# Layer 1 of a linear attention block: summing phi(K) on GpSimd and VectorE instead of TensorE

## The chip, the cores and the metric

The kernel runs on one core of a Trainium2 chip. A core has five engines with queues of their own, which work at the same time: TensorE (PE, matrix products), VectorE (DVE), ScalarE (ACT), GpSimd (POOL) and SyncE (SP, which here issues most transfers). An instruction waits for others through semaphores. The metric is the device time of one execution in microseconds (us).

## The reference

The input x has 2048 tokens of 512 values in bf16. Two layers follow each other with the same weights; each is an attention without softmax and then an MLP (F = 1792), and each of these normalises its input twice. Cut to what matters here:

```python
phi = lambda t: jnp.where(t > 0, t + 1, jnp.exp(t)) + 1e-6
pq, pk = phi(q), phi(k)                       # 32 heads of 16 values
kv = jnp.einsum("bhsd,bhse->bhde", pk, v)
z = jnp.einsum("bhsd->bhd", pk)               # sum over all 2048 tokens
num = jnp.einsum("bhqd,bhde->bhqe", pq, kv)
den = jnp.einsum("bhqd,bhd->bhq", pq, z)[..., None] + 1e-6
o = num / den                                 # then o @ wo, added to x
```

`z` is the one that the change concerns: for each of the 512 columns of phi(K), the sum over all tokens. Nothing can be divided by `den` before z is complete.

## The kernel before, in words

**Tiles and chunks.** The tokens form 16 tiles of 128 (one token per partition), and four chunks of four tiles. For each tile and layer there is a normalisation (`norm`: statistics on VectorE, a power on GpSimd, the scaling on VectorE or ScalarE), a transpose (by DMA or TensorE), and the K projection with phi (`attn_k`, L702). phi takes an exponential on ScalarE, often a relu on ScalarE too, a minimum on VectorE, and a sum or maximum on VectorE or GpSimd (L675 to L700). The result is a bf16 tile `pk` of 128 tokens by 512 columns, in one of eight buffers.

**The kv product** isn't formed from V. `attn_g_held` and `attn_g_chunk` (L767, L797) sum G, the product of phi(K) with the normalised tokens; `attn_kv` (L823) multiplies G with the V weights at the end of a layer's K phase, masks it to the heads, and multiplies it with the output weights (the M products, L853). `attn_out` (L911) then takes one product per tile of normalised phi(Q) with M.

**z** is summed in `attn_z` (L748), chunk by chunk: sixteen matmuls (L756) with a 128x128 block of a `pk` tile as the stationary operand and a single column of ones as the moving one. The PSUM result, four columns of 128 values, is copied to `zs` for chunk 0 (L762) and added to it for the others (L765). After the last chunk `zb` (L836) spreads `zs` over the head blocks for the denominators (the D matmuls, L899). In layer 1, chunks 2 and 3 divide in another layout ("tok"): for them the diagonal matrix `dz` (L841) and one matmul turn z into the row `zrow` (L788, L844).

**The order of the work** comes from a planner inside the kernel (`Scheduler`, L111). Every operation is recorded in a graph with an engine, a supposed duration in ns, a latency and a priority. The planner walks through time: for each engine it takes, of the operations that can start within a window, the one with the lowest priority value. The order it finds is then written out, engine by engine, with semaphore waits for the true dependencies, so each engine's queue is fixed. `CONF` (L348) holds the knobs: priorities by phase, `SHIFT` (additions to the priority of a group or of one operation), and `WAY` (which engine does an operation that two can do). Layer 0's MLP and layer 1's K phase are interleaved, so that TensorE has up and down projections (L955, L993) to do while tiles of layer 1 are normalised.

Of the kernel before, what the change touches and what calls it, by code (L numbers as in the profile page):

```python
# [5 lines left out]
FP32 = mybir.dt.float32  # L6
BF16 = mybir.dt.bfloat16
ACT = mybir.ActivationFunctionType
ALU = mybir.AluOpType
# [282 lines left out]
def assign_waits(graph, order, sems, dma_sems):  # L292
# [10 lines left out]
    while len(done) < total:  # L303
# [45 lines left out]
    N_HALF=1, N_K=3, N_Q=2, P_Z0=6.99, N_PB=1, N_PT=8, P_DEN=-45.12, P_A2=-16.36, P_W1=58.86, P_W2=84.95,  # L349
    P_K=47.92, P_G=125.74, P_Q=226.77, STEP=5.92, A1_Q=51.41, A1_STEP=3.23, N_H=4, N_N=2, GAP=9.92,  # L350
    TABLE_PENALTY=0.77, WINDOW=100.11,
    SHIFT={
        "B00_0": -215.0, "B00_1": -89.8, "B00_2": -26.6, "B00_3": 14.5, "B01": 170.5, "B02": 2.6,
        "B03": 342.3, "B10_0": 36.9, "B10_1": -0.2, "B10_2": 19.8, "B10_3": -16.6, "B11": 145.9, "B12": 147.7,
        "B13": 321.5, "D00": -7.7, "D01": 35.6, "D02": 71.3, "D03": 21.9, "D0_0_2": -0.8, "D0_1_3": 16.7,
        "D0_3_3": -9.4, "D10": -127.9, "D11": 5.4, "D13": 286.8, "G00_0": -37.7, "G00_1": 178.6,
        "G00_2": 70.8, "G00_3": 74.3, "G01_0": -71.1, "G01_2": -10.9, "G01_3": -70.8, "G02_0": 0.5,
        "G02_1": 195.0, "G02_2": 284.2, "G02_3": -6.8, "G03_0": 89.0, "G03_1": 18.3, "G03_2": -1.1,
        "G03_3": 584.1, "G0_0_0": 2.9, "G0_14_0": -60.7, "G0_2_0": -10.6, "G11": -2.0, "G12": 42.0,
        "G13": 28.8, "G1_1_1": -5.3, "K00_0": -245.9, "K00_1": -93.1, "K00_2": -888.1, "K00_3": -23.3,  # L360
        "K01_0": 22.0, "K01_1": 13.4, "K01_2": -187.7, "K02_1": 2.3, "K02_2": 74.6, "K02_3": -0.5,
        "K03_0": -39.1, "K03_1": -1.7, "K03_2": 123.4, "K03_3": 65.6, "K0_10": -82.3, "K10": 72.2,
        "K11": 53.6, "K12": 56.2, "K13": -41.5, "K1_1": 3.3, "K1_4": 9.5, "KV1_1": -5.4, "N00_0": -216.1,
        "N00_1": -271.1, "N00_2": -218.8, "N00_3": -3.7, "N01_0": -376.7, "N01_1": 8.9, "N01_2": -172.6,
        "N01_3": -2.9, "N02_0": -2.1, "N02_1": 63.3, "N02_2": 27.8, "N02_3": 71.9, "N03_0": 1.1,
        "N03_1": 125.2, "N03_2": 54.2, "N03_3": 25.0, "N10": -45.4, "N11": -2.3, "N13": 66.0, "O00_0": -143.2,
        "O00_1": -173.2, "O00_2": -44.0, "O00_3": -66.7, "O01": -57.3, "O02": -43.6, "O03": 41.2,
        "O10_0": -100.8, "O10_1": -47.6, "O10_2": -1.0, "O10_3": 63.4, "O11": -324.7, "O12": 0.7, "O13": 11.8,
        "OD6": 0.5, "PTA0_0": 0.7, "PTB0_2": 0.1, "Q00": 195.1, "Q01": 18.0, "Q02": 282.6, "Q03": 272.4,
        "Q10": 301.7, "Q11": -67.4, "Q12": 350.9, "Q13": 281.6, "RA1_1": 9.4, "RB0_7": -18.9, "RB0_8": -16.0,  # L370
        "RB1_1": 1.3, "TA1_6": 17.6, "TB1_8": 16.4, "U00_0": -318.5, "U00_1": -4.1, "U01": 10.6,
        "U02": -110.1, "U03": -42.4, "U10_0": -93.4, "U10_1": -26.8, "U11": -323.4, "U12": 153.7,
        "U13": 177.4, "V0": 52.4, "V1": -5.0, "W00": 6.8, "W01": 2.4, "W02": 2.5, "W03": -174.6, "W10": -38.7,
        "W10_0_10_1": -19.4, "W10_1_11_0": 4.2, "W10_2_13_0": 1.4, "W10_3_11_0": -1.7, "W11": -15.2,
        "W11_0_10_1": 3.7, "W11_0_7_0": -2.4, "W11_1_11_0": -7.7, "W11_1_7_0": 1.0, "W11_2_10_0": 46.6,
        "W11_2_2_0": 9.9, "W11_3_7_0": 3.6, "W12": -73.5, "W13": 161.9, "W20_0_0": -11.8, "W20_0_7": -1.2,
        "W20_10_7": -2.4, "W20_8_0": 0.7, "W21_12_7": 18.9, "W21_7_0": 2.2, "WO0_14_0": -4.0, "Z00": -51.5,
        "Z01": -33.6, "Z02": -104.9, "Z03": -6.4, "Z0_3": -19.5, "Z10": -0.8, "Z11": -29.8, "Z12": -111.3,
        "Z13": 2.4, "Z1_0": -3.1, "aggrA0_10": 19.5, "aggrA0_14": -16.8, "aggrA0_2": -1.3, "aggrA0_3": -2.0,
        "aggrB0_11": 3.9, "aggrB1_11": -10.5, "aggrB1_13": -0.3, "aggrB1_15": -0.8, "aggrB1_5": -3.4,  # L380
        "b20_14": -2.4, "b21_0": 3.7, "b21_13": -1.7, "b21_7": -2.8, "cpg0_0": 54.9, "expk1_10": 52.3,
        "expq0_0_3": 58.3, "expq0_1_1": 4.4, "expq1_1_0": 6.1, "expq1_2_0": -51.9, "ga1_2_1": 31.2,
        "gelu0_0_11_0": -7.1, "gelu0_0_11_1": 0.3, "gelu0_0_13_1": 2.4, "gelu0_0_1_0": 2.0,
        "gelu0_0_1_1": 1.8, "gelu0_0_4_0": -0.5, "gelu0_0_4_1": -6.4, "gelu0_0_9_1": 5.8, "gelu0_1_3_0": 7.4,
        "gelu1_0_11_0": -10.8, "gelu1_0_1_1": 3.0, "gelu1_0_6_1": -20.7, "gelu1_1_12_0": 17.2,
        "gelu1_1_8_0": 89.1, "gelu1_2_0_0": 3.3, "gelu1_3_12_0": 36.8, "gelu1_3_3_0": 16.3,
        "gelu1_3_8_0": -3.2, "ln0_1_0": 45.5, "ln1_1_2": -6.5, "minq0_0_3": 43.7, "minq0_1_1": -0.8,
        "minq1_0_2": 3.3, "normA0_4": -0.1, "normA1_9": -10.9, "normB0_12": 0.2, "normB0_13": -3.7,
        "normB0_5": 1.9, "normB0_6": 8.8, "phik0_2": -5.9, "phik1_0": -2.3, "phiq0_0_2": 7.1,
        "powA0_11": 16.1, "powA0_3": 1.3, "powA1_0": 7.6, "powA1_14": 7.5, "powA1_15": -2.7, "powA1_2": 1.9,  # L390
        "powB0_12": 20.6, "powB0_14": -34.9, "powB1_0": -14.6, "powB1_2": 17.9, "powB1_3": -7.9,
        "pr0_1_3": 2.5, "pr1_0_0": -6.8, "pr1_0_3": 9.4, "rec0_1_2": 40.6, "rec0_2_1": 58.8, "rec1_1_2": -0.9,
        "rec1_2_0": 16.6, "red1_2_3": 12.3, "reluk1_12": -1.4, "reluq0_0_1": -2.8, "reluq0_2_1": 10.4,
        "reluq1_0_0": -3.1, "statsA1_12": -5.4, "statsB0_13": -24.1, "statsB0_3": 37.2, "statsB0_6": -0.4,
        "statsB1_6": 45.8, "statsB1_7": -1.1, "vepsA0_0": -1.0, "vepsA0_12": -7.7, "vepsA0_14": -18.3,
        "vepsA0_5": 14.9, "vepsA1_12": -0.8, "vepsA1_4": 2.1, "vepsA1_8": -43.7, "vepsB1_12": 11.3,
        "vepsB1_14": 0.6, "vepsB1_3": -13.9, "vepsB1_4": -20.2, "vepsB1_5": 50.0, "vepsB1_6": -16.4,
        "w2_1": -0.9,
    },
    WAY={  # L400
        "TA0_0": "pe", "TA0_1": "pe", "TA0_10": "dma", "TA0_11": "pe", "TA0_12": "dma", "TA0_13": "dma",
        "TA0_14": "dma", "TA0_15": "dma", "TA0_2": "pe", "TA0_3": "pe", "TA0_4": "pe", "TA0_5": "pe",
        "TA0_6": "dma", "TA0_7": "pe", "TA0_8": "dma", "TA0_9": "dma", "TA1_0": "dma", "TA1_1": "dma",
        "TA1_10": "dma", "TA1_11": "pe", "TA1_12": "pe", "TA1_13": "dma", "TA1_14": "pe", "TA1_15": "dma",
        "TA1_2": "dma", "TA1_3": "dma", "TA1_4": "dma", "TA1_5": "dma", "TA1_6": "pe", "TA1_7": "pe",
        "TA1_8": "pe", "TA1_9": "dma", "TB0_0": "dma", "TB0_1": "pe", "TB0_10": "dma", "TB0_11": "dma",
        "TB0_12": "dma", "TB0_13": "dma", "TB0_14": "dma", "TB0_15": "dma", "TB0_2": "pe", "TB0_3": "dma",
        "TB0_4": "dma", "TB0_5": "dma", "TB0_6": "dma", "TB0_7": "dma", "TB0_8": "dma", "TB0_9": "dma",
        "TB1_0": "pe", "TB1_1": "dma", "TB1_10": "dma", "TB1_11": "dma", "TB1_12": "dma", "TB1_13": "dma",
        "TB1_14": "dma", "TB1_15": "dma", "TB1_2": "dma", "TB1_3": "dma", "TB1_4": "dma", "TB1_5": "dma",  # L410
        "TB1_6": "dma", "TB1_7": "dma", "TB1_8": "dma", "TB1_9": "dma", "b20_0": "dve", "b20_1": "pool",
        "b20_10": "dve", "b20_11": "pool", "b20_12": "dve", "b20_13": "pool", "b20_14": "dve",
        "b20_15": "dve", "b20_2": "pool", "b20_3": "dve", "b20_4": "pool", "b20_5": "dve", "b20_6": "pool",
        "b20_7": "pool", "b20_8": "pool", "b20_9": "pool", "b21_0": "pool", "b21_1": "pool", "b21_10": "dve",
        "b21_11": "dve", "b21_12": "pool", "b21_13": "dve", "b21_14": "pool", "b21_15": "pool",
        "b21_2": "dve", "b21_3": "pool", "b21_4": "dve", "b21_5": "dve", "b21_6": "dve", "b21_7": "pool",
        "b21_8": "dve", "b21_9": "pool", "cpg0_0": "dve", "cpg0_1": "dve", "cpg0_2": "dve", "cpg0_3": "act",
        "cpg1_0": "act", "cpg1_1": "act", "cpg1_2": "act", "cpg1_3": "act", "cpm0_0": "act", "cpm0_1": "dve",
        "cpm0_2": "dve", "cpm0_3": "act", "cpm1_0": "dve", "cpm1_1": "dve", "cpm1_2": "dve", "cpm1_3": "act",
# [36 lines left out]
def build_kernel(nc, A_x, A_wqkv, A_wo, B_x, B_w1, B_b1, B_w2, B_b2, out, conf=None, report=False):  # L456
# [5 lines left out]
    with ExitStack() as es:  # L462
# [36 lines left out]
        zb = SB("zb", [P, D], BF16)  # L499
        eps6 = SB("eps6", [P, 1], FP32)  # L500
        dz = SB("dz", [P, D], BF16)
        zrow = SB("zrow", [P, D], BF16)
        rd = SB("rd", [P, 4, H], FP32)
        rr = SB("rr", [P, 4, H], FP32)
        outb = SB("outb", [P, NOUT, D], BF16)
# [681 lines left out]
```

## Time and profile before

The time is 333.03 us, median of three runs (333.03 to 333.08). The profiled execution has a span of 331.0 us.

| engine | busy us | share | instructions |
|---|---|---|---|
| TensorE, matmuls | 324.7 | 98% | 1782 |
| TensorE, weight loads | 161.0 | 49% | 1782 |
| VectorE | 206.8 | 62% | 445 |
| ScalarE | 212.9 | 64% | 361 |
| GpSimd | 139.8 | 42% | 225 |

| group | count | busy us | mean ns |
|---|---|---|---|
| z matmuls, L756, 128 stationary columns, 1 moving column | 128 | 4.4 | 163 |
| TensorE transposes, L659 | 44 | 4.3 | 220 |
| kv products, L830 | 32 | 3.1 | 220 |
| `zs` sums on VectorE, L765 | 6 | 0.9 | 155 |
| fp32 addition of a 128x512 tile on GpSimd, L940 | 17 | 20.8 | 1230 |
| the same on VectorE, L940 | 15 | 10.7 | 719 |

Busy time is the time in which at least one of the group's instructions ran; the mean is that of a single one. Where matmuls overlap, the mean says more than one costs: 128 times 163 ns is 20.9 us, but the group was busy for 4.4. In the chain of work that ended last, each step is followed back to what released it, and its pieces are the time that each really added. TensorE's clock is full in all of the span.

### The profile page before, as it was taken

What the parts mean: (1) busy time and instruction counts of PE and PEld (TensorE: products, weight loads), DVE (VectorE), ACT (ScalarE), POOL (GpSimd) and SP (SyncE); (2) the same over time, 40 slices, a digit from 0 to 9 for tenths busy, and PEclk for the clock granted to TensorE, in tenths of its full rate; (3) what the DMA queues carried; (4) which work ended last, traced back from release to release, by engine and by line L of the source; (5) the groups of instructions that cost most, each with busy time, mean ns of one, the idle gap of its engine ahead of it and who ended that gap; (6) DMA issues with size and microseconds to landing.
All of it is one profiled execution on the core that took longest, in us unless ns stands there. A gap on an engine that the chain in (4) does not pass through costs nothing.

```text
span 331.0 us, 4842 instructions
## 1 busy us (share of the span) xinstructions
PE 324.7 (98%) x1782; PEld 161.0 (49%) x1782; DVE 206.8 (62%) x445; ACT 212.9 (64%) x361; POOL 139.8 (42%) x225
## 2 busy tenths in 40 slices
PE   7899999999999999999999999999999999999996
PEld 2444444587444444444444444448744444444444
DVE  6888848973769304997107669998899495302012
ACT  3786789999998883431940798969936521831820
POOL 6763544985847102575102642478623062600000
PEclk9999999999999999999999999999999999999999
DMA  8813750012112100212101010002332132201001
GB/s 267 272 35 67 258 201 1 18 32 50 33 35 42 21 16 2 48 32 50 32 0 34 16 32 4 1 16 50 68 77 63 32 70 75 48 2 61 4 11 54
DMA packets 40116, 18.42 MB, mean 56 GB/s; under 512 B 33756, under 2 KB 39132, under 8 KB 40092
## 3 DMA queue, kind: packets, MB, share of 16 engines
q1 hardware_dynamic: 36524, 10.90, 14.9%
q0 software_dynamic: 1056, 4.72, 4.0%
q10 hardware_dynamic: 2512, 2.49, 2.3%
q8 instruction: 14, 0.23, 0.3%
q14 instruction: 10, 0.08, 0.1%
HBM read 8.00 MB, written 2.10 MB: 31 GB/s over the span
## 4 chain that ended last, share of the span: by engine, by line
PE 93%; DVE 2%; ACT 1%; POOL 1%; DMA 1%; issue 1%
PE ps L955 29%; PE ps L993 28%; PE ps L923 8%; PE ps L710 6%; PE ps L741 6%; PE ps L807 4%; PE ps L775 3%; PE ps L728 2%; PE ps L899 2%; PE ps L756 1%; PE ps L980 1%; POOL rstd L623 1%; DMA t<-in_A_x_dram 1%; ACT eb L680 1%; DVE stats L611 1%
## 5 line engine op out<-in xcount | busy, mean ns | idle before, releaser
L961 ACT ACTIVATE gT<-ps,b1c 128x512 bf16<-128x512 f32 (+1 forms) x140 | 80.2, 603 | 38.8 <-PE ps L955 38.5
L955 PE MATMUL ps<-t,w 128*128 128x512 bf16 (+1 forms) x560 | 99.1, 336 | 0.0
L993 PE MATMUL ps<-w,gT 128*128 128x512 bf16 x434 | 97.6, 379 | 0.0
L955 PEld LDWEIGHTS ps<-t,w 128*128 128x128 bf16 x560 | 54.6, 98 | 43.3 <-ACT t L669 0.3
L993 PEld LDWEIGHTS ps<-w,gT 128*128 128x128 bf16 x434 | 42.4, 98 | 50.1
L680 ACT ACTIVATE eb<-ps 128x512 bf16<-128x512 f32 x64 | 38.4, 617 | 19.6 <-PE ps L710 16.4
L691 ACT ACTIVATE rb<-ps 128x512 bf16<-128x512 f32 x55 | 33.2, 623 | 15.5 <-PE ps L710 12.4
L623 POOL TENSOR_TENSOR rstd<-veps,neghalf 128x1 f32<-128x1 f32 x64 | 38.4, 601 | 6.6 <-DVE veps L621 1.9
L999 DVE TENSOR_TENSOR xsb<-ps,xsb 128x512 f32<-128x512 f32 x16 | 10.9, 682 | 39.0 <-PE ps L993 38.9
L1003 DVE TENSOR_TENSOR outb<-ps,xsb 128x512 bf16<-128x512 f32 x15 | 10.4, 692 | 38.4 <-PE ps L993 38.0
L611 DVE BATCH_NORM_STATS2 stats<-xsb 128x6 f32<-128x512 f32 x48 | 32.6, 680 | 0.6
L710 PE MATMUL ps<-wqkv,t 128*128 128x512 bf16 x128 | 31.6, 379 | 0.2 <-ACT t L669 0.2
L923 PE MATMUL ps<-gtb,t 128*128 128x512 bf16 x128 | 30.3, 379 | 0.0
L621 POOL TENSOR_SCALAR veps<-mv 128x1 f32<-128x1 f32 x29 | 7.7, 268 | 53.3 <-DVE mv L613 52.8
L631 ACT ACTIVATE yb<-xsb,nmr,rstd 128x512 bf16<-128x512 f32 x21 | 16.8, 811 | 20.0 <-POOL nmr L628 19.4
L907 POOL TENSOR_TENSOR t<-t,lr 128x512 bf16<-128x512 bf16 x15 | 18.1, 1212 | 16.5 <-ACT lr L903 16.5
L693 DVE TENSOR_SCALAR eb<-eb 128x512 bf16<-128x512 bf16 x55 | 20.0, 373 | 7.8 <-ACT eb L680 7.5
L741 PE MATMUL ps<-t,wqkv 128*128 128x512 bf16 x96 | 24.1, 379 | 0.0
L940 POOL TENSOR_TENSOR xsb<-xsb,b2b 128x512 f32<-128x512 f32 x17 | 20.8, 1230 | 6.3 <-ACT yb L631 3.5
L636 DVE TENSOR_SCALAR yb<-xsb,mv,rstd 128x512 bf16<-128x512 f32 x27 | 18.4, 681 | 7.8 <-POOL rstd L623 7.6
L923 PEld LDWEIGHTS ps<-gtb,t 128*128 128x128 bf16 x128 | 12.4, 98 | 15.7 <-DVE t L907 0.4
L710 PEld LDWEIGHTS ps<-wqkv,t 128*128 128x128 bf16 x128 | 12.2, 98 | 14.7 <-ACT t L669 1.0
(81 smaller groups left out, 362.2 us busy)
## 6 DMA issues: line engine op xcount, KB each, us to landing
w<-in_B_w_dram POOLq DMA_DIRECT2D x4, 896.0 KB, 7.5
out_dram<-outb SPq DMA_DIRECT2D x15, 128.0 KB, 1.7
t<-in_A_x_dram ACTq DMA_DIRECT2D x3, 512.0 KB, 8.0
t<-yb SPq DMA_TRANSPOSE x53, 2.4
wqkv<-in_A_wqkv_dram SPq DMA_DIRECT2D x1, 512.0 KB, 5.3
wqkv<-in_A_wqkv_dram ACTq DMA_DIRECT2D x1, 512.0 KB, 7.0
wqkv<-in_A_wqkv_dram POOLq DMA_DIRECT2D x1, 512.0 KB, 6.9
wo<-in_A_wo_dram POOLq DMA_DIRECT2D x1, 512.0 KB, 6.5
```

What stands on the lines that cost most here:

```text
L611: G.op("dve", lambda e: e.bn_stats(stats[:, s.slot, :], src()), 620, reads=src_keys, writes=[k + "s"], tiles=[s, *src_tiles], prio=prio, n ...
L623: G.op("pool", lambda e: e.tensor_tensor(rstd[:, s.slot:s.slot + 1], veps[:, s.slot:s.slot + 1], neghalf[:], op=ALU.pow), 570, reads=[k + ...
L680: G.op("act", lambda e: e.activation(eb[:, et.slot, :], bank(bt), ACT.Exp), 478, reads=[src_key], writes=[f"e{tag}"], tiles=[bt, et], prio ...
L691: G.op("act", lambda e: e.activation(rb[:, rt.slot, :], bank(bt), ACT.Relu), 478, reads=[src_key], writes=[f"r{tag}"], tiles=[bt, rt], pri ...
L693: G.op("dve", lambda e: e.tensor_scalar(eb[:, et.slot, :], eb[:, et.slot, :], 1.0, 1e-6, op0=ALU.min, op1=ALU.add), 210, reads=[f"e{tag}"] ...
L710: ins = e.matmul(bank(b), lhsT=yTa(yT)[:, dt, k * P:(k + 1) * P], rhs=wqkv[:, dt, D:2 * D], start=(dt == 0), stop=(dt == DT - 1))
L741: ins = e.matmul(bank(b), lhsT=wqkv[:, dt, kt * P:(kt + 1) * P], rhs=yTa(yT)[:, dt, :], start=(dt == 0), stop=(dt == DT - 1))
L923: ins = e.matmul(bank(wb), lhsT=yTa(pq)[:, kt, k * P:(k + 1) * P], rhs=gtb[:, kt, :], start=(kt == 0), stop=(kt == DT - 1))
L940: G.op("pool" if on_pool else "dve", lambda e: e.tensor_tensor(xsb[:, st, :], xsb[:, st, :], b2b[:], op=ALU.add), 1120 if on_pool else 600 ...
L955: ins = e.matmul(bank(b, n), lhsT=w1[:, dt, ft * P:(ft + 1) * P], rhs=yTa(yT)[:, dt, k0 * P:k1 * P], start=(dt == 0), stop=(dt == DT - 1))
L961: G.op("act", lambda e, ft=ft, b=b, k0=k0, k1=k1, n=n: e.activation(gT[:, g.slot, ft * 512 + k0 * P:ft * 512 + k1 * P], bank(b, n), ACT.Ge ...
L993: ins = e.matmul(bank(b), lhsT=gT[:, g.slot, ft * 512 + k * P:ft * 512 + (k + 1) * P], rhs=w2[:, ft, :], start=(ft == 0), stop=(ft == FT - 1))
```

## The change

In layer 1, z of the first three chunks (twelve tiles) no longer comes from TensorE tile by tile. The twelve `pk` tiles are added up in an fp32 tile `zacc` by eleven additions in series, `za1` to `za11`. `WAY` gives `za2`, `za3`, `za8`, `za10` and `za11` to GpSimd and the other six to VectorE. TensorE takes bf16 here, so VectorE then splits the sum in two bf16 tiles: `dz` is `zacc` rounded (the high half), and `zrow` is what the rounding left (the low half). These two tiles are free at that time. Eight one-column matmuls (`ZH`) sum both halves over the partitions, and one copy (`zsh`) puts the result into `zs`. Chunk 3 goes the old way and is added to it; so does all of layer 0. This is for taking matmuls away from TensorE.

```diff
 def attn_z(L, c, pks, prio):
     G.grp = f"Z{L}{c}"
+    if L == 1 and c < NC - 1:
+        for k in range(4):
+            st = 4 * c + k
+            if st == 0:
+                continue
+            on_pool = eng(f"za{st}") != "dve"
+            G.op("pool" if on_pool else "dve",
+                 lambda e, st=st, k=k: e.tensor_tensor(
+                     zacc[:], pkb[:, pk0s[0].slot, :] if st == 1 else zacc[:], pkb[:, pks[k].slot, :], op=ALU.add),
+                 1150 if on_pool else 600, reads=[f"pk1_{st}", "pk1_0" if st == 1 else "zacc"], writes=["zacc"],
+                 tiles=[pks[k]] + ([pk0s[0]] if st == 1 else []), prio=prio, name=f"za{st}", lat=60, fast=not on_pool)
+        if c < NC - 2:
+            return
+        G.op("dve", lambda e: e.tensor_scalar(dz[:], zacc[:], 1.0, None, op0=ALU.mult), 340, ..., name="zhi", ...)
+        G.op("dve", lambda e: e.tensor_tensor(zrow[:], zacc[:], dz[:], op=ALU.subtract), 600, ..., name="zlo", ...)
+        b = Tile(psum, "zh", "t")
+        def hfn(e):
+            for kt in range(DT):
+                for src in (dz, zrow):
+                    ins = e.matmul(bank(b)[:, kt:kt + 1], lhsT=src[:, kt * P:(kt + 1) * P], rhs=onesm[:, 0:1],
+                                   start=(src is dz), stop=(src is zrow))
+            return ins
+        G.op("pe", hfn, 300, reads=["dz", "zrow", "onesm"], writes=["zh"], tiles=[b], ..., name="ZH", lat=MM_DRAIN, n=8)
+        G.op("dve", lambda e: e.tensor_scalar(zs[:], bank(b)[:, 0:DT], 1.0, None, op0=ALU.mult), 130, ..., name="zsh", lat=40)
+        return
...
-    G.op("pe", fn, 400, reads=[f"pk{L}_{4 * c + k}" for k in range(4)] + ["onesm"], ...
+    G.op("pe", fn, 595, reads=[f"pk{L}_{4 * c + k}" for k in range(4)] + ["onesm"], ...
 def attn_kv(L, prio):
...
-        G.op("pe", fn, 220, reads=[("gt", dc), "wv"] + ...
+        G.op("pe", fn, 380, reads=[("gt", dc), "wv"] + ...
```

The last two lines change only what the planner supposes of the old z groups and of the kv products. `CONF` is replaced as a whole with it: nearly every priority, shift and choice of engine is new, so the order of all queues is another one. In counts by engine, apart from the new operations: ScalarE gets five more normalisations (28 for 23) and two more loads of its function tables (16 for 14), GpSimd loses six phi sums (17 for 23) and three residual additions (14 for 17) and gets three more products of the layer's denominators (18 for 15, L907), and VectorE gets what the others lose. The counts of all large matmuls and of TensorE transposes stay as they are. `N_H`, the number of up-projection results that the planner keeps in hand, goes from 4 to 2.

## The prediction

> **What bounds the kernel now.** I read the page first: busy time by engine and the chain that ended last. Then TensorE's waits, the busy time by stretch, and the chain in order of time where TensorE stops.
>
> ```profile
> PE 324.7 (98%) x1782; PEld 161.0 (49%) x1782; DVE 206.8 (62%) x445; ACT 212.9 (64%) x361; POOL 139.8 (42%) x225
> ...
> PE 93%; DVE 2%; ACT 1%; POOL 1%; DMA 1%; issue 1%
> ```
>
> TensorE is the bound: 98% busy and 93% of the chain. GpSimd has 191 us to spare, VectorE 124 us. So work taken from TensorE is worth its full length, and work added elsewhere is free as long as TensorE never waits for it.
>
> ```profile
> 5.62:16.13 10.51, 8.94 (x58) 4.19 (x57) 9.82 (x29) 7.21 (x14) 7.96 (x17) 1.00 0.98 305
> 16.13:39.00 22.87, 22.54 (x155) 10.95 (x153) 19.41 (x54) 17.92 (x36) 13.50 (x22) 1.00 0.35 91
> 39.00:54.00 15.00, 14.66 (x98) 7.00 (x95) 9.50 (x23) 12.94 (x24) 5.69 (x5) 1.00 0.47 171
> 54.00:199.00 145.00, 145.00 (x776) 71.79 (x775) 86.84 (x174) 102.02 (x169) 68.92 (x109) 1.00 0.14 28
> 199.00:213.00 14.00, 14.00 (x92) 7.00 (x91) 13.27 (x29) 12.14 (x22) 4.99 (x4) 1.00 0.01 2
> ```
>
> These are stretches (start and end, length, then busy time of TensorE, weight loads, VectorE, ScalarE, GpSimd). From 54 to 199 us TensorE has no gap at all, so only its amount of work counts there. Its few gaps lie in the head and where the layer-0 attention turns into its output.
>
> The chain in order of time gives the true price of each matmul, since pipelined durations overlap:
>
> ```profile
> 198.54 0.89 PE ps L807 x4
> 199.43 0.38 PE ps L756 x16
> 199.80 1.75 PE ps L807 x8
> 201.55 0.43 PE ps L899 x2
> ```
>
> A 512-column matmul takes 0.86/4 = 0.216 us. Sixteen one-column matmuls (L756, one chunk of z) take 0.38 us, and the block after them is 0.03 longer than the usual 0.86: 0.41 us, or 25.6 ns each.
>
> Now the sum. At 0.2158 us for 1315 matmuls of 512 columns, 0.109 for 252 of 256, 0.054 for 76 of 128 and 0.0256 for 128 of one column, the work after the warm-up is 318.8 us. It starts at 5.62 and ends at 328.5 us: 322.9 us, so 4.1 us are waits. About 2.25 lie before 16.13 us, 0.5 before the z matmuls at 38.59, 1.0 around the kv product (48 to 52 us), 0.3 in the second layer. A retuned order can win no more than these.
>
> **What the Trainium skill says.** "Perfetto Trace Analysis", section "Identifying the Most-Contended Engine": matmul busy time is a poor measure because matmuls are pipelined. The trace agrees: the L756 row says 163 ns each where the chain gives 25.6. "TensorE: Matmul & The Clock Gate", section "Back-to-back issue gap": 1 to 64 columns cost an issue floor of about 25 ns, and 512 columns 518 cycles (216 ns). The chain shows both. "SBUF — State Buffer", section "Who interferes with whom": a VectorE instruction with two SBUF inputs and a GpSimd instruction that reads SBUF lock each other out for a whole instruction. The trace agrees: the `dz` product (L841) took 1.64 us beside a GpSimd add running from 200.50 to 202.03, and the similar L836 took 0.68.
>
> **The change part by part.** *Removed:* three z groups of layer 1 (chunks 0 to 2), 48 one-column matmuls: 48 x 25.6 ns = 1.23 us of TensorE. *Added:* eight such matmuls for the high and low halves: 0.20. Net -1.03 us, all in a stretch without gaps, so it counts in full.
>
> *Added beside it:* eleven fp32 additions, five on GpSimd and six on VectorE. Their nearest rows:
>
> ```profile
> L940 POOL TENSOR_TENSOR xsb<-xsb,b2b 128x512 f32<-128x512 f32 x17 | 20.8, 1230 | 6.3 <-ACT yb L631 3.5 <-DVE yb L636 2.7
> L940 DVE TENSOR_TENSOR xsb<-xsb,b2b 128x512 f32<-128x512 f32 x15 | 10.7, 719 | 1.8 <-ACT yb L631 1.7
> ```
>
> That is 5 x 1.23 = 6.2 us of GpSimd and 6 x 0.72 = 4.3 us of VectorE. The rounding to `dz` is like L636 (fp32 in, bf16 out, median 0.55), the subtraction 0.72, and two small `zs` additions (0.15 each) go. VectorE gets about 5.3 us more, GpSimd 6.2. The matmuls from 100 to 199 us hide these: VectorE is 60% busy from 54 to 199, GpSimd 48%. A trace of before can't show lock-outs among the new additions; each is bounded by 0 and by one whole other instruction (1.2 us). They delay only the queue behind them, so I take 0 on TensorE and keep 1 us for the high end.
>
> *A new wait:* the eight matmuls wait for eleven additions in series, the rounding and the subtraction. In the changed instruction order they stand behind the last K projection, and the four K blocks that include tile 11 are well ahead. Between them lie 16 G, 16 Q, then 16 more matmuls of G, K, G and Q: 48 x 0.216 = 10.4 us. After the K of tile 11: exp and minimum 0.6 + 0.3, its phi addition 1.2, the last two sums 2.4, rounding and subtraction 1.3, some 6 us with semaphores. Slack about 4 us: no wait. Queued behind the eight are Q and G matmuls, with all TensorE behind them.
>
> *Moved:* the whole order, since priorities and engine choices are new (and the planner's costs of Z and KV are raised). Layer 0's end: the z wait of 0.5 us goes, as more K and Q matmuls stand before Z. The first kv product stands behind all G and one Q block, not between G matmuls, so its wait shrinks from 1.0 to some 0.2. Against that, the M products are followed at once by the output projection; a copy out of PSUM takes 0.69 us plus about 0.3 of drain and signals, with 0.87 us of matmuls between: up to 0.5 of wait. Net -0.8. Layer 1's end: all four copies of M are on VectorE (4 x 0.68 in series), which leaves the fourth some 0.4 us late: +0.3. In its favour, `dz` no longer has GpSimd phi additions queued beside it. VectorE, 95% busy from 199 to 213, may run late: 0 to 1.5 us, I take 0.2. Elsewhere ScalarE gets five more normalisations (0.81 each) less two evacuations (0.6 each), 2.8 us, and two more table loads (1.28 each); from 54 to 131 us it is already 67 of 77 us busy. I take no wait there and keep 1 us for the range. Head and tail keep their order nearly: 0.
>
> Sum: -1.03 - 0.8 + 0.3 + 0.2 = -1.3 us, so 333.03 - 1.3 = 331.7 us.
>
> **The rivals.** *More of the waits go (330.4).* If the new order also wins 1.3 us of the head's 2.25 or loses nothing at the M copies, 331.7 - 1.3. For it: the head's waits are on normalisation and evacuation, which moved engines. Against: the first ten groups on TensorE are the same. *The work goes and waits take its place (332.9).* -1.03, with 0.9 us of new waits beyond the old ones at the layer 1 turn: no change. For it: VectorE has 0.7 us left of 14 there. Against: `zs` needs only one chunk's 16 matmuls then, as before. *Slower (334.5).* An engine beside TensorE becomes the bound in a stage: ScalarE with its table loads from 54 to 131 us, or VectorE at the turn with the sums locked out by GpSimd. Worked out: -1.03 + 1.0 (ScalarE) + 1.5 (VectorE) = +1.5. For it: 87% and 95% busy. Against: TensorE waits for neither before 199 us, at the same loads.
>
> **How the numbers follow.** Forecast 0.52, more waits gone 0.15, no change 0.17, slower 0.16. The 0.2% line lies at 332.36 and 333.70. Faster takes nearly all of the first two: 0.66; same 0.18; slower 0.16. The range 330.2 to 333.9 leaves out the far half of the slower case and the end of the better one.
>
> **What would show it.** In the changed profile the z matmuls should number 88, not 128 (eighty at the old line and eight new), and the chain should show no wait before the eight. TensorE should stay at 98 or 99%, gapless from 54 to 199 us. The kv product's wait should fall below 0.4 us, and a wait of 0.3 to 0.5 should show at the first output projection of each layer. The new sums should take 1.15 to 1.3 us on GpSimd and 0.65 to 0.75 on VectorE. Wrong would be: TensorE waiting on ScalarE during the up projection, on `zrow` at the eight matmuls, or on `zb` or `dz` at the turn, by over 1 us together. Then the order, not the z work, decides the time.

## The result, and the profile after

After the change the kernel takes 336.46 us (median of six runs, 334.97 to 337.14), before it 333.03 (six runs, 332.87 to 333.14): a ratio of 1.0095, 95% interval 1.007 to 1.012. It is slower by 3.4 us where 1.3 less was forecast, and the time lies outside the range.

The page of after: busy time by engine, TensorE's granted clock in 40 slices, and the chain that ended last.

```profile
PE 326.5 (97%) x1742; PEld 160.9 (48%) x1742; DVE 214.5 (64%) x455; ACT 217.5 (65%) x366; POOL 138.1 (41%) x227
...
PEclk9999799999999999999999999999999999999999
...
PE 86%; ACT 8%; DMA 2%; DVE 1%; issue 1%; POOL 1%
```

TensorE has forty matmuls fewer, as meant (1742 for 1782). But a DMA now has 2% of the chain, about 7 us, and one slice, 34 to 42 us, has a lower clock; before, no slice had. TensorE's waits name the DMA:

```profile
PE ps L711 <- DMA t<-yb: 2.8, 1, 2.8
...
PE ps L954 <- ACT gtb L819: 0.2, 1, 0.2
```

A K projection (L711) of layer 0 waits 2.8 us for a DMA transpose; before, TensorE waited for no DMA. In order of time, TensorE alone:

```profile
34.37 1.03 PE L711 MATMUL ps<-wqkv,t 128*128 128x512 bf16 x4
38.16 3.57 PE L711 MATMUL ps<-wqkv,t 128*128 128x512 bf16 x8 [2.77 <-DMA t<-yb]
41.53 1.93 PE L742 MATMUL ps<-t,wqkv 128*128 128x512 bf16 x8
```

Start to start, the first four matmuls take 3.79 us instead of 0.86: 2.9 of wait. The next eight take 3.37 instead of 1.73: 1.6 more, from the low clock. That is 4.5 us in one place. The same stretch by windows (busy time of TensorE, weight loads, VectorE, ScalarE, GpSimd; then TensorE's clock, the DMA engines' share, GB/s):

```profile
34.00:36.00 2.00, 1.40 (x7) 0.43 (x5) 1.93 (x5) 1.58 (x4) 1.11 (x2) 1.00 1.21 372
36.00:38.00 2.00, 0.00 (x0) 0.00 (x0) 1.04 (x3) 0.52 (x2) 0.83 (x1) 1.00 0.88 274
38.00:40.00 2.00, 1.83 (x5) 0.72 (x6) 0.00 (x0) 0.00 (x0) 0.30 (x1) 0.55 1.06 397
40.00:42.00 2.00, 2.00 (x7) 0.68 (x5) 0.29 (x1) 1.31 (x3) 0.00 (x0) 0.60 0.98 332
42.00:44.00 2.00, 2.00 (x11) 0.94 (x10) 1.33 (x5) 2.00 (x5) 0.00 (x0) 1.00 1.04 352
```

The clock of a window is a mean: it was 0.50 from 38.2 to 41.6 us and full on both sides. All engines run dry, while the DMA engines are full. What fills them is the four loads of the MLP weights `w1` and `w2`, 896 KB each, from GpSimd's queue. GpSimd in order of time, first before, then after (L580 and L581 are the same line):

```profile
34.27 1.53 POOL L580 DMA_DIRECT2D w<-in_B_w_dram  x2 [2.97 <-ACT t L669]
35.82 1.16 POOL L697 TENSOR_TENSOR pkb<-eb,rb 128x512 bf16<-128x512 bf16 x1
36.92 1.91 POOL L580 DMA_DIRECT2D w<-in_B_w_dram  x2
```

```profile
30.57 1.53 POOL L581 DMA_DIRECT2D w<-in_B_w_dram  x2
32.11 1.16 POOL L698 TENSOR_TENSOR pkb<-eb,rb 128x512 bf16<-128x512 bf16 x1
33.20 1.90 POOL L581 DMA_DIRECT2D w<-in_B_w_dram  x2
```

Before, the loads waited 3 us for the copy of a TensorE transpose (L669); after, they wait for nothing and start 3.7 us earlier. The last DMA transpose (tile 13) is issued at 30.99, that is behind the first load (30.57) and ahead of the other three. The transposes of 26 to 42 us, issue to landing (shortest, median, longest), before and after:

```profile
DMA to landing us min/median/max: 2.4/2.5/2.5
```

```profile
DMA to landing us min/median/max: 2.5/2.5/7.0
```

The code says why. In layer 0 only the last transpose of each chunk, tiles 3, 7, 11 and 15, goes into the list `trs` that the loads wait for:

```python
for c in range(NC):
    for k in range(4):
        ...                      # tr = transpose of tile 4c+k, by TensorE or DMA
    trs.append(tr)
...
late(f"w1_{h}", ..., trs)        # and w2: wait for all of trs
```

`WAY` decides who transposes. Before, tile 11 was on TensorE, came late, and so held the loads until the transposes of tiles 14 and 13, which the list does not hold, had landed. The change gives tile 11 to a DMA and tile 8 to TensorE. The counts stay the same; the accidental hold is gone.

### The profile page after: what moved, and what is told of

It reads as the page before. It is cut to its first block, busy times and chain, and to the rows that moved or that the text cites. A ratio compares the mean times of both kernels' runs of the same rounds, so it can differ in the third digit from the quotient of the medians.

```text
span 335.1 us, 4774 instructions
## 1 busy us (share of the span) xinstructions
PE 326.5 (97%) x1742; PEld 160.9 (48%) x1742; DVE 214.5 (64%) x455; ACT 217.5 (65%) x366; POOL 138.1 (41%) x227
## 4 chain that ended last, share of the span: by engine, by line
PE 86%; ACT 8%; DMA 2%; DVE 1%; issue 1%; POOL 1%
PE ps L986 29%; PE ps L1024 28%; PE ps L711 6%; PE ps L954 6%; PE ps L838 4%; PE ps L742 4%; PE ps L806 3%; DMA t<-yb 2%; PE ps L729 2%; ACT eb L681 2%; PE ps L596 1%; ACT yb L632 1%; ACT rb L692 1%; ACT lr L932 1%; PE ps L930 1%; ACT lr L934 1%
## 5 line engine op out<-in xcount | busy, mean ns | idle before, releaser
L632 ACT ACTIVATE yb<-xsb,nmr,rstd 128x512 bf16<-128x512 f32 x23 | 18.5, 808 | 41.3 <-POOL nmr L629 39.0
L624 POOL TENSOR_TENSOR rstd<-veps,neghalf 128x1 f32<-128x1 f32 x64 | 38.2, 597 | 6.8 <-DVE veps L622 1.9
L711 PE MATMUL ps<-wqkv,t 128*128 128x512 bf16 x128 | 32.7, 394 | 3.0 <-DMA t<-yb 2.8
L694 DVE TENSOR_SCALAR eb<-eb 128x512 bf16<-128x512 bf16 x54 | 16.9, 319 | 23.4 <-ACT eb L681 22.9
L954 PE MATMUL ps<-gtb,t 128*128 128x512 bf16 x128 | 31.2, 379 | 0.2 <-ACT gtb L819 0.2
L938 POOL TENSOR_TENSOR t<-t,lr 128x512 bf16<-128x512 bf16 x18 | 21.6, 1199 | 18.6 <-ACT lr L934 18.6
L617 POOL TENSOR_SCALAR veps<-mv 128x1 f32<-128x1 f32 x32 | 7.0, 219 | 50.5 <-DVE mv L614 48.7
L622 POOL TENSOR_SCALAR veps<-mv 128x1 f32<-128x1 f32 x29 | 8.1, 278 | 41.8 <-DVE mv L614 41.2
L1030 DVE TENSOR_TENSOR xsb<-ps,xsb 128x512 f32<-128x512 f32 x16 | 10.9, 681 | 18.0 <-PE ps L1024 17.9
L711 PEld LDWEIGHTS ps<-wqkv,t 128*128 128x128 bf16 x128 | 12.5, 100 | 19.2 <-issue 4.9
L637 DVE TENSOR_SCALAR yb<-xsb,mv,rstd 128x512 bf16<-128x512 f32 x25 | 17.6, 703 | 4.7 <-POOL rstd L624 4.4
L959 DVE TENSOR_TENSOR xsb<-ps,xsb 128x512 f32<-128x512 f32 x16 | 10.7, 683 | 15.1 <-PE ps L954 15.1
```

The source lines that it names most:

```text
L624: G.op("pool", lambda e: e.tensor_tensor(rstd[:, s.slot:s.slot + 1], veps[:, s.slot:s.slot + 1], neghalf[:], op=ALU.pow), 570, reads=[k + ...
L632: G.op("act", lambda e: e.activation(yb[:, y.slot, :], src(), ACT.Identity, bias=nmr[:, s.slot:s.slot + 1], scale=rstd[:, s.slot:s.slot + 1]),
L711: ins = e.matmul(bank(b), lhsT=yTa(yT)[:, dt, k * P:(k + 1) * P], rhs=wqkv[:, dt, D:2 * D], start=(dt == 0), stop=(dt == DT - 1))
L938: lambda e, kt=kt, r=r: e.tensor_tensor(yTa(pq)[:, kt, :], yTa(pq)[:, kt, :], lr[:, r.slot, :], op=ALU.mult),
L954: ins = e.matmul(bank(wb), lhsT=yTa(pq)[:, kt, k * P:(k + 1) * P], rhs=gtb[:, kt, :], start=(kt == 0), stop=(kt == DT - 1))
```

## The experiments

The theory: the early weight loads cost it all. They make tile 13's transpose land late, TensorE waits, and its clock falls. The rivals: the new z costs time itself (sums late or locked out, VectorE overloaded), or the low clock has another cause than the wait. In all kernels below the order of every queue and every buffer is kept as it was in the kernel started from, but for the edit named.

**Loads early in the kernel before.** `trs` without tile 11:

```diff
-            trs.append(tr)
+            if c != 2:
+                trs.append(tr)
```

> The kernel before with its order and buffers kept; only the loads of the MLP weights no longer wait for the transpose of tile 11, the one that TensorE does last. Theory A: the loads are issued some 3 us earlier, the last transposes by DMA take several us longer, the K projections of the last tiles wait 2 to 3 us, and the time rises to 335 to 337 us. Rival B: the loads come earlier with no effect, 333.0 us.

338.39 us (336.7 to 339.84), ratio 1.0146 [1.0116, 1.0176]. TensorE's waits, and the transposes' landing, of this kernel:

```profile
PE ps L966 <- DMA t<-yb: 3.9, 1, 3.9
```

```profile
DMA to landing us min/median/max: 2.4/2.5/7.7
```

The old kernel with nothing but the loads 3.1 us earlier shows the same wait, the same late landing, and a clock of 0.50 from 40 to 42 us. It needs neither the new z nor the new order. The wait is longer and the time higher than expected (2 to 3 us, 335 to 337); 0.9 us of it are a wait for another transpose, at 230 us, which the kernel before doesn't have; the run with the new z for two chunks, below, says more of such transposes.

**Loads late in the kernel after.** `trs.append(tr)` moves into the inner loop, so that the loads wait for all sixteen transposes:

```diff
-            trs.append(tr)          # once per chunk
+                trs.append(tr)      # for every tile
```

> The changed kernel with every queue's order and every buffer as it is; only the four loads of the MLP weights wait for all transposes of layer 0 instead of for one of each chunk. Theory A (the loads start some 3.7 us earlier than before and slow the last transposes, TensorE idles 2.9 us for one and then runs at a low clock): the wait of the K projection falls from 2.8 us to under 0.4, the clock is full in all runs, and the time is 335.0 (the runs of the changed kernel at full clock) - 2.9 = 332.1 us, below the kernel before. Rival B (the added sums and the moved evacuations cost the time): the transposes land earlier, but the time stays above 335.

333.38 us (333.02 to 333.86), ratio 0.9998 [0.9989, 1.0008], full clock in all runs. All transposes land in 2.5 us and the wait for the DMA is gone: some 3.2 us come back. But a gain against before doesn't appear. The waits, GpSimd's queue and one VectorE instruction show another cost:

```profile
PE ps L967 <- DVE pkb L943: 1.2, 1, 1.2
```

```profile
33.66 1.52 POOL L837 DMA_DIRECT2D w<-in_B_w_dram  x2 [3.23 <-DMA t<-yb]
35.21 1.16 POOL L954 TENSOR_TENSOR pkb<-eb,rb 128x512 bf16<-128x512 bf16 x1
36.30 1.91 POOL L837 DMA_DIRECT2D w<-in_B_w_dram  x2
```

```profile
34.28 2.25 DVE L941 TENSOR_SCALAR eb<-eb 128x512 bf16<-128x512 bf16 x1
```

The loads wait 3.2 us at the head of GpSimd's queue, and the phi sum of tile 10 behind them starts at 35.21 instead of 32.11. There it runs beside VectorE's minimum of tile 11 (L941), which ends only when that sum has ended (36.37), after 2.25 us. So the maximum behind it (L943) comes late, and with it the PSUM bank for which TensorE waits. That all this comes of the waiting loads is so far a reading; the second experiment below tests it.

**The wait filled with matmuls.** The kernel after with twelve matmuls of 512 columns, whose result is not used, put ahead of the K projection that waits:

```diff
+        def fill(e):
+            for _ in range(12):
+                ins = e.matmul(bank(fb), lhsT=onesm[:, 0:P], rhs=onesm[:, :], start=True, stop=True)
+            return ins
```

> The changed kernel with twelve extra matmuls of 512 columns on TensorE (2.6 us, results unused) ahead of the K projection that waits 2.8 us for its transpose; all else in its order. If the low clock after the wait comes of TensorE standing idle: no run shows a clock below full, the wait shrinks to some 0.3 us, and the time is that of the changed kernel's runs at full clock, 335.0 us. If the clock drops for another reason (the moment in the run, the transfers): the clock of 0.995 and times over 336 stay in most runs.

334.97 us (334.41 to 335.21), ratio 1.0045 [1.003, 1.006]. The transpose still lands after 6.9 us, but the clock is 0.999 to 1.0 in all eight runs, and the eight K matmuls take their usual 1.73 us:

```profile
34.85 2.75 PE L1336 MATMUL ps<-onesm 128*128 128x512 bf16 x12
37.56 1.90 PE L968 MATMUL ps<-wqkv,t 128*128 128x512 bf16 x8
39.29 1.89 PE L999 MATMUL ps<-t,wqkv 128*128 128x512 bf16 x8
```

So the low clock comes of TensorE's idleness and not of the DMA traffic. Against after (1.0095) it is 0.5% less: about 1.7 us, with an interval of 1.0 either way, is the price of the clock over all six runs of after; the trace of one that had it said 1.6.

**Loads late, and behind the phi sum.** The kernel with late loads, with the four loads placed behind the phi sum of tile 10 in GpSimd's queue:

```diff
-  w1_0  w1_1  phik0_10  w2_0  w2_1
+  phik0_10  w1_0  w1_1  w2_0  w2_1
```

> The changed kernel with the late weight loads of the first experiment, and the four loads put behind GpSimd's phi sum of tile 10 in its queue instead of around it. Theory: in the first experiment the loads' own wait held that sum up, so that a PSUM bank came free late and TensorE waited 1.2 us for it; moved, this wait goes. 333.4 - 1.3 = 332.1 us, 0.3% below the kernel before, the clock full. Rival (the rest of the new order eats what z gives): 333.0 to 333.4, no difference from the kernel before.

332.30 us (331.8 to 332.61), ratio 0.9976 [0.9967, 0.9984]: faster than both kernels. TensorE's waits, but for the warm-up's:

```profile
PE ps L916 <- DVE yb L893: 1.4, 2, 0.9
PE ps L1117 <- DVE gtb L1078: 0.2, 1, 0.2
PE ps L1210 <- ACT gtb L1075: 0.2, 1, 0.2
```

And the minimum of tile 11, with the phi sum out of its way:

```profile
33.84 0.29 DVE L941 TENSOR_SCALAR eb<-eb 128x512 bf16<-128x512 bf16 x1
```

The 1.2 us went, so the reading was right: a load that waits holds everything behind it on its queue, and what it holds up can collide with other work when it comes. From after to here it is 1.2%, 4.0 us with an interval of 0.9 either way; the trace of after had 4.5 in the wait and the clock.

**The old z in that kernel.** The branch of the new z is switched off, all else stays:

```diff
-            if L == 1 and c < NC - 1:
+            if False:
```

> The same kernel as the one with the loads behind the phi sum, and only the new z undone: 48 one-column matmuls back on TensorE, the eleven sums, the split and the eight matmuls out, their z sums taken at once so that no bank is held. The difference of the two is the price of z at full clock. By the chain of the kernel before: 1.03 us slower than that kernel. If the added sums cost TensorE anything: less than 0.7 us slower, or faster.

333.88 us (333.24 to 334.01), ratio 1.0018 [1.001, 1.0026]. Without the new z it is 0.42% slower: 1.4 us, with an interval of 0.4 either way. 1.03 us are the forty matmuls; the waits show where the rest can come from, a wait ahead of the Q products that stand behind an old z group:

```profile
PE ps L998 <- DVE zs L1052: 0.3, 1, 0.3
```

It is 0.4 us start to start. I gave chunk 1's old z group PSUM bank 6, which the next Q product needs, so these Q products wait until the `zs` addition has read it. This wait is of my making: without it the difference is about 1.0 us, what the forty matmuls cost. The added sums cost TensorE nothing that shows.

**The old z in the kernel after**, with the same edit:

> The changed kernel with its order and buffers kept, and only the sum of phi(K) undone: the eleven additions, the split and the eight matmuls are out, the 48 one-column matmuls of the first three chunks are back on TensorE (chunk 2's where the eight stood). If the new z is worth its matmuls (1.0 us) and adds no wait: 1.0 us slower than the changed kernel, 336.0 us at full clock and 337.5 else. Rival B (the additions hold up VectorE and GpSimd and so TensorE): faster than the changed kernel by 1 us or more.

338.71 us (336.93 to 339.26), ratio 1.0144 [1.0119, 1.0168]. It too is slower than with the new z, but the same Q products wait 1.2 us here for the same bank, since VectorE does the `zs` addition behind other work. So the size says nothing of the z work; the kernel above is the cleaner answer.

**The new z in the kernel before.** The new code and choices of engine for the sums, the old order otherwise:

> The kernel before, its order kept, with the new z of twelve tiles put in (each addition where its operands are ready). In that order the K projection of tile 11 is one of the last, so the series of sums ends late: theory says that the eight matmuls, and behind them the sums of z and the denominators, come some 4 us late and TensorE waits 2 to 4 us: 334 to 336 us. If the series of sums hides anywhere: 332.0.

337.37 us (336.56 to 338.38), ratio 1.0133 [1.011, 1.0155]. That is more than the 334 to 336 expected. In this order the K of tile 11 is one of the last, and the series of sums ends late. The chain in order of time, and the window around it:

```profile
199.56 1.20 POOL zacc L1017
...
200.84 1.23 POOL zacc L1017
...
202.55 0.70 DVE zrow L1025
...
203.30 0.35 PE ps L1032 x8
203.66 1.53 PE ps L1095 x4
```

```profile
199.00:213.00 14.00, 11.54 (x73) 5.17 (x73) 12.31 (x22) 8.74 (x17) 5.67 (x5) 0.88 0.01 2
```

TensorE waits 2.2 us for `zrow`. Behind that it doesn't wait but runs slowly: the four G products take 1.53 us instead of 0.86. The clock, 0.88 over this window, was 0.50 from 203.7 to 207.2 us, and this costs another 1.7; here the DMA engines are all but idle (2 GB/s). A further 1.1 us is a wait for a transpose at 157 us. -1.0 + 2.2 + 1.7 + 1.1 is 4.0 us, and 4.4 were measured, with an interval of 0.7. So the new z can lose more than it saves where the sums end late; the order of after, which has the K of tile 11 early, avoids that.

**The new z for chunks 0 and 1 only, in the kernel before**, so that nothing waits for tile 11 (chunks 2 and 3 go the old way):

```diff
-    if L == 1 and c < NC - 1:
+    if L == 1 and c < NC - 2:
```

> The kernel before, its order kept, with the new z for chunks 0 and 1 alone (eight tiles: seven additions, all long done when they are needed); chunks 2 and 3 the old way. 32 matmuls go and eight come: 24 x 25.6 ns = 0.6 us, so 332.5 us if z is worth its matmuls in this order too; 333.1 or more if the additions cost TensorE time.

334.39 us (333.98 to 335.22), ratio 1.0043 [1.0029, 1.0057]: the expected gain failed to appear. The waits show why:

```profile
PE ps L1243 <- DMA t<-yb: 1.2, 1, 1.2
...
PE ps L1044 <- DVE zs L1036: 0.3, 1, 0.3
```

24 matmuls fewer are 24 x 25.6 ns = 0.6 us. Thanks to them TensorE comes to the up projection of chunk 3 (L1243) at 156.9 us instead of 157.6. The last transpose that this needs isn't late in its start (154.60; before 154.72), but it lands after 3.4 us, at 158.03, where the kernel before has 2.5 and 157.17. -0.6 + 1.2 + 0.4 for the second row (start to start) is +1.0 us; 1.4 were measured, with an interval of 0.5.

No large load runs beside this transpose, but the traces show what does: one 16 KB packet of a DMA queue of the kind that the page calls "instruction", at 155.13 us. The kernel before has such a packet at 149.42 and none beside these transposes. The slow transpose of the run above (157 us) and the one at 230 us in the kernel before with early loads have one beside them too. In all eleven traces, leaving out the first 20 us and the transposes issued from 30 to 32 us, 57 transposes take over 2.75 us, and each has a packet of 8 or 16 KB of such a queue in flight; of the 532 that have none, the longest takes 2.56. This goes together in every trace; no run moved the packets alone, so that they are the cause isn't shown.

**Three blocks moved ahead of the remaining waits.** The kernel that was fastest, with a Q block ahead of a TensorE transpose of layer 0's output, another ahead of layer 1's first output projection, and a denominator product (`D0_2_1`) ahead of layer 0's:

```diff
-  M0_2 ... WO0_0_0 ... D0_2_1        PTB0_1 ... Q0_3_2        WO1_0_0 ... Q1_3_2
+  M0_2 ... D0_2_1 WO0_0_0            Q0_3_2 PTB0_1            Q1_3_2 WO1_0_0
```

> The version with the weight loads behind the phi sum of tile 10 took 332.3 us and leaves waits of 0.30 us at the last TensorE transpose of layer 0's output, about 0.35 at layer 1's first output projection and 0.2 ahead of the denominators. Here three Q or denominator blocks are moved ahead of these three places. If those waits are plain latency of a copy that more matmuls can hide, they go: 331.6 us, up to 0.7 below that version, ratio to before about 0.995. Rival: the moved blocks find their own data or banks late and the wait only changes place: 332.3, ratio 0.9976.

332.50 us (332.13 to 332.97), ratio 0.9979 [0.9971, 0.9987]: no better. The wait at the transpose is gone. The third wait stays at 0.3 us: in both traces it lies ahead of the last M product, in front of the place where the Q block was put. And at layer 0's output projection

```profile
PE ps L1186 <- ACT gtb L1075: 0.7, 1, 0.7
```

the denominator product moved in front now waits 0.7 us for the same copies, where the projection had waited 0.2. There the rival held: the wait changed its place and grew. The kernel gives this product PSUM bank 6, the bank of the last M product, which one of those copies empties. That this is why it waits is the likeliest reading, but was not tried apart.

## Why the prediction was wrong, point by point

- **The step that failed:** the part "Moved". It gives terms to the ends of the two layers and to ScalarE, and settles the rest with "Head and tail keep their order nearly: 0." Layer 0's K phase, up to the z wait at 38.59, had no term at all. I had compared the order on TensorE and found it nearly the same; what the DMA queues wait for was not compared. A transpose's move between engines, which stood in the diff, changed what four large loads wait for. This cost 4.5 us by the trace (2.9 of wait, 1.6 of clock), and holding the loads back gave 4.0 ± 0.9 back. None of the rivals had it: they looked for a slower case in ScalarE and VectorE only.
- **z, -1.03:** right. Undoing it alone measured 1.4 ± 0.4, of which 0.4 are the wait that I caused. 88 matmuls of one column remain, and the eight start with no wait, as forecast. Their slack was 2.0 us, not 4: `zrow` ends at 200.07 and they start at 202.08. Both sides of that sum were off: 52 matmuls (11.2 us) stand between, not 48, and from the K of tile 11 to the end of `zrow` it took some 9 us, not 6.
- **The new sums:** these are the rows of after (count: shortest, median, longest ns; first and last start):

```profile
L760 POOL TENSOR_TENSOR zacc<-zacc,pkb x5: 1153/1154/1157, 116.8 to 196.5; 128x512 f32<-128x512 f32 x5
L760 DVE TENSOR_TENSOR zacc<-zacc,pkb x5: 675/684/692, 158.7 to 184.6; 128x512 f32<-128x512 f32 x5
L760 DVE TENSOR_TENSOR zacc<-pkb x1: 1018/1018/1018, 114.6 to 114.6; 128x512 f32<-128x512 bf16 x1
L766 DVE TENSOR_SCALAR dz<-zacc x1: 1371/1371/1371, 197.9 to 197.9; 128x512 bf16<-128x512 f32 x1
```

  Ten of eleven lie in the forecast bounds. The first on VectorE takes 1.02: a GpSimd product runs from 113.92 to 115.08, and the sum starts at 114.61. The rounding (L766) takes 1.37 where 0.55 was forecast and 0.43 measured in the old order: a GpSimd phi sum runs beside it from 197.65 to 198.99. The Trainium skill, "SBUF — State Buffer", section "Who interferes with whom", has a lock of the ports that the two engines share, for a VectorE instruction with two SBUF inputs and for some modes of one like the rounding; both durations fit it. As forecast, none of it reaches TensorE.
- **Layer 0's turn, -0.8:** about -0.3 in the trace of after. The z wait of 0.5 went, the kv wait fell by some 0.6, the output projection waits 0.38 start to start (0.3 to 0.5 forecast) and 0.13 more at its second product; a further 0.3 at the first TensorE transpose behind it was not forecast.
- **Layer 1's turn, +0.3, and VectorE late, +0.2:** +0.1 to +0.4 in the traces of after and of the fastest variant, so the size was right. But the wait stands ahead of the last M product and not, as forecast, at the first output projection, and the trace puts it down to ScalarE (`lr`), not to VectorE's copies.
- **ScalarE no bound:** right. From 54 to 131 us it is busy for 61.7 of 77 us, before for 67.2, and TensorE idles only 0.4 us there in all. All of it lies at layer 0's output projection and the transpose behind it.
- **The sum.** Without the early loads the change was measured at 332.30, against 332.93 in the same runs: -0.24%, or -0.8 us ± 0.3, where -1.3 was forecast. The rest of the change, with the old z in its place, was 0.6 us ± 0.3 slower than before; 0.4 of that is the wait that I caused. So the new order gained nothing that shows, where -0.3 was forecast. Differences of this size can't be traced to one place: the first TensorE transposes start anywhere from 5.6 to 6.2 us in the profiles of these kernels. The clock is part of that, for it isn't full from the start: the eleven warm-up matmuls begin 0.43 us apart, twice the usual, until 4.9 us before and to their end after. (By the prediction's own figures TensorE's work is 318.6 us, not 318.8; nothing rests on it.)

## What to carry to other kernels

When a change moves an operation to another engine, look for everything that waits for that operation, transfers above all: a large load whose start depends on it moves too, and hits whatever small transfer is then in flight. A wait may protect something that its dependency doesn't name; before counting a lost wait as a gain, ask what it kept apart, and put the waiting load behind the work on its queue that others need. A transfer with little slack can turn a gain into a loss without any fault of the change: compare its landing in both traces before blaming the change.

## What the runs showed of the hardware

- A 128x512 DMA transpose that lands in 2.5 us by itself took 6.7 to 7.7 us beside the weight loads (274 to 397 GB/s in the windows of after). The Trainium skill, "DMA: Bandwidth & Descriptors", section "Issuing engines are not separate DMA queues", says that all transfers end on the same sixteen engines and interleave; the trace fits, with transposes from SyncE's queue and loads from GpSimd's.
- Transposes with a packet of 8 or 16 KB of an instruction queue in flight beside them took up to 4.8 us; without one, and away from the weight loads of layer 0, none took over 2.6. That the packets are the cause isn't shown.
- After 2.8 us without a matmul TensorE's clock was at 0.50 for 3.41 us, which cost another 1.6 us; in two of six runs of after the clock stayed full, and these were the fastest (334.97 and 335.12, against 336.32 to 337.14). The same 3.41 us at 0.50 followed pauses of 3.9, 2.4 and 2.2 us in three of the experiments. Pauses of 1.2 us left the clock full. The Trainium skill, "TensorE: Matmul & The Clock Gate", section "Part 1: The HAM clock gate", has a half clock after an idle window of about 3.4 us, which runs free of the kernel's start. The length of the slow stretch and the falls in only some runs fit that window; that 2.2 us are enough is shorter than the page's length.
- Matmuls that fill such a wait keep the clock up: twelve of them were worth 1.7 ± 1.0 us.
